# Retention followed by a leaky-ReLU MLP on one core: the front of the kernel, up to the second token group, written in another order

## The chip, the cores and the metric

The kernel runs on one core of a Trainium2 chip. The metric is device time in microseconds (us) of one execution. The profiler's trace of one execution gives the start and length of each instruction on five engines: TensorE (PE, with its weight loads shown apart as PEld), VectorE (DVE), ScalarE (ACT), GpSimd (POOL) and SyncE (SP, which here only issues DMAs). PEclk is the share of PE's full clock that was granted.

## The reference: what is computed

q, k and v are float32 tensors of 8 batches, 8 heads, 576 positions and 64 dimensions. Each head has a decay gamma. The first half is a retention layer, the second an MLP over the 4608 tokens of 512 channels:

```python
scores = scale * np.matmul(q, k.transpose(0, 1, 3, 2))
Dmat = np.where(rel >= 0, gamma[:, None, None] ** rel[None, :, :], 0.0)
ret = scores * Dmat[None, :, :, :]
return np.matmul(ret, v).astype(np.float32)
...
h = x @ w_in                      # 512 -> 2048
g = np.maximum(0.01 * h, h)
return (g @ w_out).astype(np.float32)    # 2048 -> 512
```

`rel` is the distance of two positions. x is the retention's output with the heads side by side.

## The kernel before, in words

**Units and groups.** The 4608 tokens are 36 units of 128 tokens (two chunks of 64), and 9 groups of four units (512 tokens). A batch has nine chunks, so unit 4 lies across two batches and its loads come in two halves. For a unit the kernel

- loads k, q and v with `load(u)`: three DMAs of 256 KB (pieces of 256 bytes), six of half the size for a unit across batches, into one of six sets of buffers `t32`;
- casts them to float16, q and v times decay tables (`cast_k` L165 on ACT, `cast_q` L168 and `cast_v` L172 on DVE or POOL), into `qk16` and `v16`;
- transposes k and q to `qkT`: on PE through PSUM (`transpose_pe` L193, copied out at L200 by `transposed`) for units below NPE, by a DMA on SP (`transpose_dma` L176) for later ones;
- multiplies k with q inside each chunk, and k with v for the state (`scores`, L208 and L217, 16 matmuls of 64 by 64 each, into the single PSUM tile `sc`);
- masks the scores to float16 (`masks`, L226 on DVE), adds the chunk's state to the running one (`state`, L248, L250, or L253 and L254 where the state is scaled, on DVE) and casts that to float16 (`state_cast`, L266 and L269);
- computes two output parts (`outputs`, L284 from the masked scores and L295 from the state before), 32 matmuls into different places of the single PSUM tile `ot`; `own` (L306, ACT) copies the first part to SBUF and `add` (L314, DVE) adds the second to it and writes `xT`, the MLP's input.

**The MLP of a group.** Layer 1 (L327) multiplies by `w_in` and writes g through the leaky ReLU on ACT (L341). `h_half` does two blocks of 128 hidden channels for 256 tokens, `h_block` one block for 512. Layer 2 of group 0 is `wide` (L369): 16 pieces of four 512-column matmuls, four pieces for each quarter of `w_out`. Layer 2 of the other groups is `seven` (L429), a Strassen-like scheme of seven products of 16 matmuls with 256 columns. It needs sums of weights (`mix_weights`, L394, four of them in two halves, once) and sums of g (`mix`, L413, four in two halves for each group), both on DVE. In it, `keep` (L441, L443) and `give` (L452, L454) move PSUM out, and a dictionary of hooks says what is recorded behind which product.

**What sets the order.** The order is written out by hand: each engine executes its instructions in the order in which the code records them, and a wait holds all that stands behind it on that engine. That holds for DMAs too: SP issues the unit loads, the stores and the transposes in one order, and POOL issues the weight loads (which cast to float16) between its casts. Weights come as four pieces of `w_in` (`load_w_in`, two DMAs each) and four of `w_out` (`load_w_out`). A list of earlier DMAs given as `after` makes a load wait for them. Before, the chain is: w_in 0 after unit 2 is loaded, unit 4 after w_in 2, w_out 0 after q of unit 4, unit 5 after w_out 0, w_out 2 after q of unit 5, unit 6 after w_out 2.

**The stages.** The opening (units 0 to 3), layer 1 of group 0, layer 2 of group 0 with units 4 and 5, group 1 with units 6 to 12, and then groups 2 to 8. `burst(u)` records scores of unit u and outputs of u-1, and `ahead(u)` casts and transposes a unit by DMA. `step(u)` is a burst, the load of a later unit and `ahead(u + 2)`. In groups 2 to 7 four steps lie between layer-1 blocks and products. `keep_warm` (L495) issues matmuls on zeros. They give no result.

Of the kernel before, what the change touches and what calls it, by code (L numbers as in the profile page):

```python
# [18 lines left out]
def kernel(  # L19
# [23 lines left out]
    NPE = 10  # L43
# [75 lines left out]
    def load(u, after=None):  # L119
        for x in (1, 0, 2):  # L120
# [4 lines left out]
            for j, rows in ((0, P),) if same else ((0, CH), (1, CH)):  # L125
                b, w = (c + j) // CB, (c + j) % CB
                d = nc.sync.dma_start(
# [173 lines left out]

    owns = {}
# [7 lines left out]
    def add(u):  # L310
        g, t0 = u // 4, (u % 4) * P
        if g not in xT:
            xT[g] = x_pool.tile([P, NP, TOK], F16, name="xT")
        nc.vector.tensor_tensor(  # L314
            out=xT[g][:, :, t0 : t0 + P].rearrange("q (c g) t -> q c g t", g=2),
            in0=ot_tiles[u][:, :, NP : 2 * NP].rearrange("q g (c j) t -> q c g (j t)", j=2),
            in1=owns[u].rearrange("q (c g) j t -> q c g (j t)", g=2),
            op=ADD,
        )
# [28 lines left out]
    def h_half(g, a, fb):  # L348
# [4 lines left out]
        leaky(g_tile(g)[:, 2 * fb : 2 * fb + 2, ts], hps)  # L353

# [150 lines left out]
    def prepare(u):  # L505
        cast_k(u)
        transpose_pe(u, 1)
        transposed(u, 1, nc.scalar.copy)
        cast_q(u, nc.vector)
        transpose_pe(u, 0)  # L510
        transposed(u, 0, nc.scalar.copy)
        cast_v(u, nc.gpsimd)

    def settle(u):
        state(u, 0)
        state_cast(u, nc.scalar.copy, (0,))
        masks(u)

    def settle_rest(u):
        state(u, 1)  # L520
        state_cast(u, nc.gpsimd.tensor_copy, (1,))
# [6 lines left out]
    prepare(0)  # L528
    scores(0)
    settle(0)  # L530
    w_in_loads = []
    for u in range(1, 4):
        cast_k(u)
        transpose_pe(u, 1)
        transposed(u, 1, nc.scalar.copy)
        cast_q(u, nc.vector)
        settle_rest(u - 1)
        keep_warm(2)
        transpose_pe(u, 0)
        transposed(u, 0, nc.scalar.copy)  # L540
        cast_v(u, nc.gpsimd)
        finish(u - 1)
        if u == 2:
            w_in_loads.append(load_w_in(0, (last_load[2, 2],)))
        if u == 3:
            w_in_loads.append(load_w_in(1))
        scores(u)
        settle(u)
        keep_warm(3)
    settle_rest(3)  # L550
    w_in_loads.append(load_w_in(2))
    w_in_loads.append(load_w_in(3))


    def halves(g, *items):
        for a, fb in items:
            h_half(g, a, fb)

    load(4, w_in_loads[2])
    o_loads = [load_w_out(0, (last_load[4, 0],)), load_w_out(1)]  # L560
    load(5, o_loads[0])
    o_loads += [load_w_out(2, (last_load[5, 0],)), load_w_out(3)]

    halves(0, (0, 0), (0, 1))
    finish(3)
    halves(0, (0, 2), (0, 3), (1, 0), (1, 1), (1, 2), (1, 3), (0, 4), (0, 5), (1, 4), (1, 5))
    load(6, o_loads[2])
    load(7)
    cast_k(4)
    cast_q(4, nc.vector)  # L570
    cast_v(4, nc.gpsimd)
    halves(0, (0, 6), (0, 7))
    transpose_pe(4, 1)
    transposed(4, 1, nc.scalar.copy)
    transpose_pe(4, 0)
    transposed(4, 0, nc.vector.tensor_copy)
    halves(0, (1, 6), (1, 7))
    scores(4)
    settle(4)
    settle_rest(4)  # L580
# [6 lines left out]
    load(8)  # L587
    wides((0, 1), (1, 1))
    cast_k(5)
    cast_q(5, nc.vector)  # L590
    cast_v(5, nc.gpsimd)
    wides((2, 1),)
    transpose_pe(5, 1, sc_pool)
    transposed(5, 1, nc.scalar.copy)
    transpose_pe(5, 0, sc_pool)
    transposed(5, 0, nc.vector.tensor_copy)
    wides((3, 1), (0, 2))
    scores(5)
    outputs(4)
    settle(5)  # L600
    settle_rest(5)
    own(4)
    add(4)
    wides((1, 2), (2, 2), (3, 2))
    load(9)
    finish(5)
    wides((0, 3), (1, 3), (2, 3), (3, 3))


    load(10)  # L610
    cast_k(6)
    cast_q(6, nc.vector)
    cast_v(6, nc.gpsimd)
    halves(1, (0, 0), (0, 1))
    transpose_pe(6, 1)
    transposed(6, 1, nc.scalar.copy)
    transpose_pe(6, 0)
    transposed(6, 0, nc.vector.tensor_copy)
    halves(1, (0, 2), (0, 3))
    scores(6)  # L620
    settle(6)
    settle_rest(6)
    cast_k(7)
    cast_q(7, nc.vector)
    cast_v(7, nc.gpsimd)
    load(11)
    halves(1, (0, 4))
    transpose_pe(7, 1)
    transposed(7, 1, nc.scalar.copy)
    transpose_pe(7, 0)  # L630
    transposed(7, 0, nc.vector.tensor_copy)
    halves(1, (0, 5))
    scores(7)
    outputs(6)
    settle(7)
    settle_rest(7)
    own(6)
    add(6)
    halves(1, (0, 6), (0, 7))
    finish(7)  # L640

    def pe_casts(u):
        cast_k(u)
        cast_q(u, nc.vector)
        cast_v(u, nc.gpsimd)

    def pe_transposes(u):
        transpose_pe(u, 1, sc_pool)
        transposed(u, 1, nc.scalar.copy)
        transpose_pe(u, 0, sc_pool)  # L650
        transposed(u, 0, nc.vector.tensor_copy)

    def burst(u):
# [3 lines left out]
        if u - 1 >= 8:  # L657
            outputs(u - 1)
        if u < NU:
# [3 lines left out]
            state_cast(u, nc.gpsimd.tensor_copy)  # L663
        if u - 1 >= 8:
# [3 lines left out]
    def ahead(u):  # L668

        if u < NPE or u >= NU:  # L670
            return
# [9 lines left out]
    pe_casts(8)  # L681
    pe_transposes(8)
    halves(1, (1, 0), (1, 1))
    burst(8)
    ahead(10)
    mix_weights(0, 0)
    mix_weights(0, 1)
    halves(1, (1, 4), (1, 5))
    pe_casts(9)
# [78 lines left out]
```

## Time and profile before

| | us |
|---|---|
| median of three runs (323.5 to 326.23) | 323.84 |
| the profiled execution | 323.91 |
| its span on the core | 322.1 |
| opening, to the first layer-1 matmul of group 0 | 23.4 |
| group 2 starts, in the chain of waits | 117.2 |
| one steady group | 29.1 |

The span runs from the first to the last instruction. The rest of an execution's time lies around it. In the table of windows a row is a stretch of the span: its length, then for each engine busy time with the number of instructions, then the granted clock, the mean busy share of the 16 DMA engines (which can come out over 1) and the GB/s that they wrote. In a timeline row an engine name with a q (SPq) is its queue of DMA issues, and the bracket says how long the engine had been idle and what ended that. In rows of groups the number before the comma is us in total, the one behind it the mean of one in ns, and behind the bars stands the idle time ahead of the group. In the page's part on DMA queues, q0 holds the DMAs that POOL issues, q1 those of SP; the numbers are packets, MB written and share of the 16 engines' time.

### The profile page before, as it was taken

The numbers are of one execution on the slowest core, as the hardware profiler recorded it, in microseconds if no ns is written. First come the engines' busy times: TensorE is split into PE (matmuls) and PEld (weight loads), VectorE is DVE, ScalarE is ACT, GpSimd is POOL, SyncE is SP. The second block draws the span as 40 slices with busy tenths as digits, with TensorE's granted clock in tenths as the row PEclk, the third lists the DMA queues.
The fourth block names the chain that finished last, engine by engine and source line by source line (L and its number), as shares of the span: only waits on it lengthen the run. The fifth ranks groups of instructions, "written<-read, shape, count | busy, mean of one in ns | idle before, by whom it ended". The sixth has DMA issues, their size and how long they took to land.

```text
span 322.1 us, 9343 instructions
## 1 busy us (share of the span) xinstructions
PE 283.8 (88%) x4063; PEld 192.1 (60%) x4063; DVE 171.9 (53%) x288; ACT 145.7 (45%) x255; POOL 94.7 (29%) x114
## 2 busy tenths in 40 slices
PE   2777926998757799999999999999999999999995
PEld 1345822456546664785487468647845874685474
DVE  1651002165599964783585457468636846661252
ACT  4553730136644227625732762476167237514710
POOL 1163105012257432342335333332533433000000
PEclk9997985999999999999999999999999999999999
DMA  8959698999054979769847976896597673003003
GB/s 184 220 75 174 129 207 134 222 263 243 2 132 93 190 172 242 168 137 263 184 107 166 258 166 135 163 285 156 122 263 158 147 192 123 2 4 132 0 0 132
DMA packets 149770, 49.49 MB, mean 154 GB/s; under 512 B 140640, under 2 KB 145376, under 8 KB 149728
## 3 DMA queue, kind: packets, MB, share of 16 engines
q1 hardware_dynamic: 145152, 44.58, 59.2%
q0 software_dynamic: 4288, 4.20, 8.6%
q8 instruction: 32, 0.52, 0.7%
q10 hardware_dynamic: 288, 0.11, 0.1%
q14 instruction: 10, 0.08, 0.1%
HBM read 36.81 MB, written 9.44 MB: 144 GB/s over the span
## 4 chain that ended last, share of the span: by engine, by line
PE 75%; DVE 9%; DMA 7%; ACT 3%; issue 3%; POOL 1%; SPq 1%; DVEq 0%; POOLq 0%; ACTq 0%
PE acc L327 33%; PE acc L429 28%; PE acc L369 5%; DMA t<-in_q_dram 4%; PE sc L208 2%; DMA w_in<-in_moe_w_in_dram 2%; DMA w_out<-in_moe_w_out_dram 2%; DVE w_mix L394 2%; PE sc L217 1%; PE acc L193 1%; PE ot L284 1%; PE ot L295 1%; DVE mix L413 1%; ACT qkT L200 1%; DVE s L250 1%
## 5 line engine op out<-in xcount | busy, mean ns | idle before, releaser
L327 PE MATMUL acc<-xT,w_in 128*128 128x512 f16 (+1 forms) x704 | 131.5, 344 | 2.4 <-DMA w_in<-in_moe_w_in_dram 2.4
L341 ACT ACTIVATE gt<-acc 128x512 f16<-128x512 f32 x144 | 86.1, 598 | 66.4 <-PE acc L327 64.8
L327 PEld LDWEIGHTS <-w_in 128*128 128x128 f16 x704 | 68.0, 99 | 55.9 <-issue 2.9
L429 PEld LDWEIGHTS <-gt 128*128 128x128 f16 x640 | 61.9, 98 | 13.1 <-issue 4.0
L226 DVE TENSOR_TENSOR s<-sc,cs 128x512 f16<-128x512 f32 x36 | 24.7, 686 | 46.3 <-PE sc L217 46.2
L429 PE MATMUL acc<-w_out,gt 128*128 128x256 f16 x384 | 45.9, 273 | 2.7 <-DVE v L443 1.8
L172 POOL TENSOR_TENSOR v<-t,cs 128x512 f16<-128x512 f32 x36 | 40.7, 1132 | 6.1 <-DMA t<-in_v_dram 6.1
L306 ACT COPY own<-ot 128x512 f32<-128x512 f32 x36 | 21.1, 586 | 45.9 <-PE ot L295 38.4
L266 POOL CAST st<-s 128x512 f16<-128x512 f32 x21 | 12.8, 611 | 93.7 <-DVE s L250 56.9
L429 PE MATMUL acc<-w_mix,gt 128*128 128x256 f16 x256 | 30.7, 273 | 1.0 <-DVE w_mix L394 1.0
L314 DVE TENSOR_TENSOR xT<-ot,own 128x512 f16<-128x512 f32 x36 | 24.6, 685 | 11.8 <-ACT own L306 11.7
L413 DVE TENSOR_TENSOR mix<-gt 128x1024 f16<-128x1024 f16 x16 | 15.0, 937 | 28.8 <-ACT gt L341 28.8
L429 PE MATMUL acc<-w_mix,mix 128*128 128x256 f16 x256 | 29.3, 273 | 0.0
L168 POOL TENSOR_TENSOR qk<-t,cs 128x512 f16<-128x512 f32 x26 | 28.5, 1095 | 0.0
L269 POOL CAST st<-s 128x256 f16<-128x256 f32 x15 | 6.9, 460 | 69.4 <-DVE s L254 29.0
L429 PEld LDWEIGHTS <-mix 128*128 128x128 f16 x256 | 25.1, 98 | 2.9
L165 ACT CAST qk<-t 128x512 f16<-128x512 f32 x36 | 22.3, 620 | 7.8 <-DMA t<-in_k_dram 7.8
L217 PE MATMUL sc<-v,qk 64*64 64x64 f16 x576 | 11.4, 198 | 8.9 <-POOL v L172 8.9
L250 DVE TENSOR_TENSOR s<-sc,s 128x256 f32<-128x256 f32 x40 | 16.7, 418 | 3.1 <-PE sc L217 2.6
L193 PEld LDWEIGHTS <-qk 128*128 128x128 f16 x80 | 6.0, 109 | 19.6 <-ACT qk L165 13.3
L208 PEld LDWEIGHTS <-qkT 64*64 64x64 f16 x576 | 8.4, 110 | 14.6 <-issue 12.3
L369 PE MATMUL acc<-w_out,gt 128*128 128x512 f16 x64 | 16.5, 417 | 0.0
(45 smaller groups left out, 216.8 us busy)
## 6 DMA issues: line engine op xcount, KB each, us to landing
out_dram<-osb SPq DMA_DIRECT2D x17, 512.0 KB, 3.2
t<-in_k_dram SPq DMA_DIRECT2D x32, 256.0 KB, 3.9
t<-in_q_dram SPq DMA_DIRECT2D x32, 256.0 KB, 4.3
t<-in_v_dram SPq DMA_DIRECT2D x32, 256.0 KB, 4.5
w_in<-in_moe_w_in_dram POOLq DMA_DIRECT2D x8, 256.0 KB, 5.1
w_out<-in_moe_w_out_dram POOLq DMA_DIRECT2D x4, 512.0 KB, 6.8
t<-in_k_dram SPq DMA_DIRECT2D x8, 128.0 KB, 3.3
t<-in_q_dram SPq DMA_DIRECT2D x8, 128.0 KB, 3.9
```

The source lines that it names most:

```text
L165: nc.scalar.copy(out=qk16[u][:, 1], in_=t32[u, 1])
L168: eng.tensor_tensor(out=qk16[u][:, 0], in0=t32[u, 0], in1=decay(u, 0), op=MUL)
L172: eng.tensor_tensor(out=v16[u], in0=t32[u, 2], in1=decay(u, 1), op=MUL)
L226: nc.vector.tensor_tensor(out=s16s[u], in0=sc_tiles[u][:, :, 0], in1=mask_sb.unsqueeze(1).unsqueeze(1).to_broadcast([P, 2, NP, CH]), op=MUL,)
L250: nc.vector.tensor_tensor(out=to, in0=st, in1=carry[0], op=ADD)
L306: nc.scalar.copy(out=owns[u], in_=ot_tiles[u][:, :, 0:NP].rearrange("q j c t -> q c j t"))
L314: nc.vector.tensor_tensor(out=xT[g][:, :, t0 : t0 + P].rearrange("q (c g) t -> q c g t", g=2), in0=ot_tiles[u][:, :, NP : 2 * NP].rearrang ...
L327: nc.tensor.matmul(out=hps[:, n, :], lhsT=w_in16[:, c, f * P : (f + 1) * P], rhs=xT[g][:, c, ts], start=(c == 0), stop=(c == NP - 1),)
L341: nc.scalar.activation(out=out, in_=in_, func=mybir.ActivationFunctionType.Lrelu)
L369: nc.tensor.matmul(out=ys[tb], lhsT=g_t[0][:, f, tb * P : (tb + 1) * P], rhs=w_out16[:, f, :], start=(f == 0), stop=(f == NF - 1),)
L413: nc.vector.tensor_tensor(out=z[:, fs], in0=a[:, fs], in1=b[:, fs], op=op)
L429: nc.tensor.matmul(out=r[name][:, tb, :], lhsT=lhs[:, f, tb * P : (tb + 1) * P], rhs=rhs[:, f, :], start=fresh and n == 0, stop=f == HF - ...
```

## The change

**Loads.** Units 0 to 3 stay on SP. Units 4 to 7 are issued by POOL (`load` takes an engine), in one row with the weights: w_in 3, unit 4, w_out 0 and 1, unit 5, w_out 2 and 3, units 6 and 7. The explicit order among the loads is gone but for unit 8, which waits for v of unit 6. POOL gives up the v casts of units 4 to 7, which go to DVE. w_in 0 to 2 are issued inside the opening, each behind the second state cast of its unit.

The two fences show POOL's order from the v cast of unit 3 to that of the next unit that POOL casts. `t_1`, `t_0` and `t_2` are buffers of k, q and v, the number behind them tells the tile.

Before:
```order
L172 TENSOR_TENSOR v_418<-t_2_129,cs 128x512
L143 DMA w_in_97<-in_moe_w_in_dram 64x4x512 x2
L269 CAST st_492<-s_491 128x256
L143 DMA w_in_97<-in_moe_w_in_dram 64x4x512 x4
L149 DMA w_out_98<-in_moe_w_out_dram 128x4x512 x4
L172 TENSOR_TENSOR v_700<-t_2_515,cs 128x512
```
Now:
```order
L172 TENSOR_TENSOR v_405<-t_2_129,cs 128x512
L269 CAST st_389<-s_388 128x256
L143 DMA w_in_97<-in_moe_w_in_dram 64x4x512 x2
L269 CAST st_493<-s_492 128x256 x2
L143 DMA w_in_97<-in_moe_w_in_dram 64x4x512 x2
L127 DMA t_1_504<-in_k_dram 64x8x64 x2
L127 DMA t_0_507<-in_q_dram 64x8x64 x2
L127 DMA t_2_510<-in_v_dram 64x8x64 x2
L149 DMA w_out_98<-in_moe_w_out_dram 128x4x512 x2
L127 DMA t_1_571<-in_k_dram 128x8x64
```
The cast of `v_700` (unit 4), which stood behind all four w_out loads, is no longer on POOL, and unit loads (L127) stand between the weights. Units 5 to 7 and the other w_out follow in the same way, and POOL's next cast is q of unit 8.

**Opening.** A unit's transposes are recorded ahead of the outputs of the unit before, k of the next unit is cast one step earlier, and both state casts are on POOL. The outputs of units 0 to 3 go through `outputs_acc`: both parts are accumulated in the same place of PSUM, with a drain of PE between the matmuls that read the lower and the upper 64 partitions, and one copy on ACT (`x_copy`) writes `xT`. `own` and `add` are gone for these units.

**Layer 2 of group 0 and group 1.** State casts of units 4 to 7 are both on ACT. `mix_weights` is moved up from group 1 (five halves in layer 2 of group 0, three early in group 1). Units 8 and 9 are transposed by DMA (NPE 8). In group 1 the tokens of units 6 and 7 get layer 1 by `h_unit`: four blocks of 128 channels for 128 tokens. Four steps (9 to 12) hang in `seven(1)`, behind products 0, 2, 4 and 6, where two steps (11 and 12) hung behind products 0 and 4, and a step loads unit u + 4 in place of u + 3.

ACT's order around the casts of k of units 6 (`qk_1019`, now `qk_1012`) and 7 (`qk_1121`, now `qk_1127`), before:
```order
L165 CAST qk_1019<-t_1_685 128x512
L341 ACTIVATE gt<-acc 128x2x256 x2
L200 COPY qkT<-acc 128x512
L341 ACTIVATE gt<-acc 128x2x256 x2
L269 CAST st_1112<-s_1111 128x256
L165 CAST qk_1121<-t_1_691 128x512
L341 ACTIVATE gt<-acc 128x2x256
L200 COPY qkT<-acc 128x512
```
Now:
```order
L165 CAST qk_1012<-t_1_679 128x512
L380 ACTIVATE gt<-acc 128x2x256 x2
L200 COPY qkT<-acc 128x512
L380 ACTIVATE gt<-acc 128x2x256 x3
L269 CAST st_1118<-s_1117 128x256 x2
L165 CAST qk_1127<-t_1_685 128x512
L200 COPY qkT<-acc 128x512
L380 ACTIVATE gt<-acc 128x2x256
```
Two state casts stand ahead of the cast of k of unit 7, and no layer-1 block lies between that cast and the copy of its transposes.

DVE's order at the end of `seven(1)`, from the first sum `v` (L443, now L490) to the add of unit 11 (the last L314, now L353), before:
```order
L443 TENSOR_TENSOR v<-acc,u_1804 128x512
L454 TENSOR_TENSOR osb<-acc,v 128x2x256
L226 TENSOR_TENSOR s_1910<-sc,cs 128x512
L250 TENSOR_TENSOR s_1912<-sc,s_1744 128x256
L253 TENSOR_TENSOR stmp<-sc,s_1912 128x256
L254 TENSOR_TENSOR s_1912<-stmp,cs 128x256
L314 TENSOR_TENSOR xT<-ot,own 128x4x128
L454 TENSOR_TENSOR osb<-acc,u_1804 128x2x256 x2
```
Now:
```order
L490 TENSOR_TENSOR v<-acc,u_1668 128x512
L501 TENSOR_TENSOR osb<-acc,v 128x2x256
L226 TENSOR_TENSOR s_1865<-sc,cs 128x512
L250 TENSOR_TENSOR s_1867<-sc,s_1738 128x256
L250 TENSOR_TENSOR s_1867<-sc,s_1867 128x256
L353 TENSOR_TENSOR xT<-ot,own 128x4x128
L501 TENSOR_TENSOR osb<-acc,u_1668 128x2x256 x2
L226 TENSOR_TENSOR s_1990<-sc,cs 128x512
L250 TENSOR_TENSOR s_1992<-sc,s_1867 128x256
L253 TENSOR_TENSOR stmp<-sc,s_1992 128x256
L254 TENSOR_TENSOR s_1992<-stmp,cs 128x256
L353 TENSOR_TENSOR xT<-ot,own 128x4x128
```
The last burst's masks, states and add came ahead of the last two `osb` sums and now stand behind them. The first layer-1 matmul of group 2 reads what the last row writes.

The diff, cut:

```diff
-    NPE = 10
+    NPE = 8
-    def load(u, after=None):
+    def load(u, eng=None, after=None):
...
-                d = nc.sync.dma_start(
+                d = (eng or nc.sync).dma_start(
...
+    def outputs_acc(u):
+        ot = ot_pool.tile([P, 2, 2 * NP, CH], FP, name="ot")
+        ot_tiles[u] = ot
+        to = ot[:, 0].rearrange("q (c j) t -> q c j t", j=2)
+        seen = set()
+        for r in range(2):
+            if r:
+                nc.tensor.drain()
+            for c in range(NP):
+                for o in range(2):
+                    h = c + NP * o
+                    nc.tensor.matmul(
+                        out=to[half(o), c, r, :], lhsT=v16[u][half(r), h, :],
+                        rhs=s16s[u][half(r), h % 2, h // 2, :],
+                        start=o not in seen, stop=False, skip_group_check=True,
+                    )
+                    seen.add(o)
+            for j in range(2):
+                if (2 * u + j) % CB == 0:
+                    continue
+                for c in range(r, NP, 2):
+                    for o in range(2):
+                        nc.tensor.matmul(
+                            out=to[half(o), c, j, :],
+                            lhsT=st_before(u, j)[half(r), (c + NP * o) // 2, :],
+                            rhs=qkT[u][half(r), 0, (c + NP * o) // 2, half(j)],
+                            start=False, stop=True, skip_group_check=True,
+                        )
+    def x_copy(u):
+        nc.scalar.copy(
+            out=x_of(u), in_=ot_tiles[u][:, 0].rearrange("q (c j) t -> q c (j t)", j=2)
+        )
...
+    def h_unit(u, fb):
+        g, t0 = u // 4, (u % 4) * P
+        ts = slice(t0, t0 + P)
+        hps = acc_pool.tile([P, 4, P], FP, name="acc")
+        for n in range(4):
+            h_mm(hps, n, g, 4 * fb + n, ts)
+        leaky(g_tile(g)[:, 4 * fb : 4 * fb + 4, ts], hps)
...
+    for u in range(3):
+        n = u + 1
+        state(u, 0)
+        state_cast(u, pool_copy, (0,))
+        transpose_pe(n, 1)
+        transposed(n, 1, act_copy)
+        keep_warm(1)
+        cast_q(n, nc.vector)
+        masks(u)
+        state(u, 1)
+        cast_v(n, nc.gpsimd)
+        state_cast(u, pool_copy, (1,))
+        load_w_in(u)
+        transpose_pe(n, 0)
+        transposed(n, 0, act_copy)
+        keep_warm(2)
+        outputs_acc(u)
+        x_copy(u)
+        if n < 3:
+            cast_k(n + 1)
+        keep_warm(1)
+        scores(n)
+        if u:
+            keep_warm(2)
...
+    load_w_in(3)
+    load(4, nc.gpsimd)
+    load_w_out(0)
+    load_w_out(1)
...
+    halves(1, (0, 3), (0, 4))
+    scores(6)
+    settle(6)
+    pe_casts(7)
+    turn(7, 1)
+    halves(1, (0, 5))
+    turn(7, 0)
+    ahead(8)
+    load(10)
...
-    seven(1, {0: [lambda: step(11)], 1: [rest_of_weights], 4: [lambda: step(12)]})
+    seven(
+        1,
+        {
+            0: [lambda: step(9)],
+            2: [lambda: step(10)],
+            4: [lambda: step(11)],
+            6: [lambda: step(12)],
+        },
+    )
```

`turn(u, x)` is the two PE transposes calls of before in one function, `settle(u)` records both chunks' states, state casts (ACT) and the masks, `pe_casts(u)` the three casts.

244 lines of the change are left out of this document (95 added, 149 removed).

## The prediction

> **What bounds the kernel now.** I read the page first, for where TensorE (PE) is not busy, then a table of stages, then who waits inside the bad stages, then the DMA.
>
> ```profile
> span 322.1 us, 9343 instructions
> ...
> PE   2777926998757799999999999999999999999995
> ...
> PEclk9997985999999999999999999999999999999999
> ...
> q1 hardware_dynamic: 145152, 44.58, 59.2%
> q0 software_dynamic: 4288, 4.20, 8.6%
> ```
>
> The span is 322.1 us. The 40 slices are about 8 us each: from slice 16 on PE is full, and the holes and the low clocks lie in the first fifteen, up to about 117 us. The table of windows puts numbers on the stages: the opening, layer 1 of group 0, the hole, layer 2 of group 0, all of group 1, then one steady group.
>
> ```profile
> core 0: us, PE busy (x) PEld busy (x) DVE busy (x) ACT busy (x) POOL busy (x), PEclk, DMA share, GB/s
> 0.00:23.38 23.38, 13.21 (x271) 7.73 (x271) 9.79 (x22) 11.29 (x21) 8.03 (x15) 1.00 0.77 163
> 23.38:42.60 19.22, 17.03 (x184) 14.18 (x185) 3.07 (x6) 10.89 (x20) 4.31 (x7) 0.91 0.90 149
> 42.60:51.90 9.30, 0.36 (x16) 0.30 (x16) 0.00 (x0) 0.99 (x2) 2.55 (x3) 0.67 0.92 163
> 51.90:70.03 18.13, 17.46 (x175) 7.94 (x168) 6.42 (x12) 2.58 (x5) 3.10 (x4) 0.89 1.08 223
> 70.03:117.19 47.16, 35.29 (x691) 29.09 (x690) 38.46 (x60) 21.01 (x38) 18.82 (x19) 1.00 0.66 145
> 117.19:146.30 29.11, 29.07 (x433) 19.36 (x432) 17.05 (x30) 14.95 (x26) 11.20 (x14) 1.00 0.80 184
> ```
>
> A steady group costs 29.11 us with PE busy for 29.07 of it, so group 2 onward is bound by PE, and the change leaves that alone. Group 1 takes 47.16 us, with PE idle for 11.9. Between 42.60 and 51.90 PE does 0.36 us of work. The timeline tells why:
>
> ```profile
> 44.08 0.58 SPq L127 DMA_DIRECT2D t<-in_q_dram  x1
> 48.93 1.48 POOL L149 DMA_DIRECT2D w_out<-in_moe_w_out_dram  x2 [9.49 <-DMA t<-in_q_dram]
> 50.42 1.06 POOL L172 TENSOR_TENSOR v<-t,cs 128x512 f16<-128x512 f32 x1
> 51.54 0.43 PE L217 MATMUL sc<-v,qk 64*64 64x64 f16 x16 [8.95 <-POOL v L172]
> 51.90 8.23 PE L369 MATMUL acc<-w_out,gt 128*128 128x512 f16 x28
> ```
>
> PE waits 8.95 us for POOL's cast of v of unit 4. POOL is held in front of it by w_out loads that wait for a load of unit 5. PE then runs cold (clock 0.67 and 0.89 in these two stages). So the end is set by PE, and what can be won is PE's waits before 117.
>
> **The change part by part.** I rebuild the front by hand, with durations from these rows (the chain of waits, then groups by form, then DMA by window).
>
> ```profile
> 66.85 3.56 PE acc L369 x16
> 70.41 1.75 PE acc L327 x16
> 72.15 0.45 PE acc L193 x8
> 107.89 4.19 DVE w_mix L394 x4
> 113.53 3.65 PE acc L429 x32
> 117.19 4.32 PE acc L327 x20
> ```
> ```profile
> L172 POOL TENSOR_TENSOR v<-t,cs 128x512 f16<-128x512 f32 x36 | 40.7, 1132 | 6.1 <-DMA t<-in_v_dram 6.1
> L226 DVE TENSOR_TENSOR s<-sc,cs 128x512 f16<-128x512 f32 x36 | 24.7, 686 | 46.3 <-PE sc L217 46.2
> L314 DVE TENSOR_TENSOR xT<-ot,own 128x512 f16<-128x512 f32 x36 | 24.6, 685 | 11.8 <-ACT own L306 11.7
> L165 ACT CAST qk<-t 128x512 f16<-128x512 f32 x36 | 22.3, 620 | 7.8 <-DMA t<-in_k_dram 7.8
> L306 ACT COPY own<-ot 128x512 f32<-128x512 f32 x36 | 21.1, 586 | 45.9 <-PE ot L295 38.4 <-DVE osb L454 5.4
> L250 DVE TENSOR_TENSOR s<-sc,s 128x256 f32<-128x256 f32 x40 | 16.7, 418 | 3.1 <-PE sc L217 2.6
> L143 POOL DMA_DIRECT2D w_in<-in_moe_w_in_dram x8 | 5.1, 650 | 0.0
> L149 POOL DMA_DIRECT2D w_out<-in_moe_w_out_dram x4 | 3.0, 755 | 19.9 <-DMA t<-in_q_dram 19.9
> L269 ACT CAST st<-s 128x256 f16<-128x256 f32 x7 | 2.8, 404 | 8.7 <-DVE s L250 6.7 <-DVE s L248 1.2 <-DVE s L254 0.8
> ```
> ```profile
> 2.00:14.00 12.00, 6.02 (x117) 3.73 (x117) 3.78 (x8) 5.69 (x11) 2.44 (x3) 1.00 1.05 239
> 26.00:32.00 6.00, 4.16 (x24) 3.10 (x25) 0.69 (x1) 1.62 (x3) 1.53 (x3) 0.73 1.14 174
> 62.00:70.00 8.00, 8.00 (x129) 3.80 (x127) 4.35 (x8) 1.99 (x4) 1.40 (x2) 1.00 1.12 253
> ```
>
> *DMA.* A unit is 0.786 MB in float32: 3.3 us at 239 GB/s, 3.1 at 253. Half a million weights land as 0.524 MB of float16: 3.0 us at 174 GB/s, for each of the eight weight pieces. With all of it in order and no gaps: units 0 to 3 from 2.0 take 13.2 us, to 15.2. The new order issues w_in 0 and 1 at about 11 and 16 (each behind POOL's state cast of its unit), beside the loads of units 2 and 3. By the shares and counts above a packet of the hardware queue costs 21 ns (59.2% of 322.1 us on 16 engines over 145152 packets) and one of the software queue, so far weights alone, 103. No row shows the two queues loaded together, so unit 3 lands between 15.2 (weights last) and 21.2 (both pieces first); I take 21.2, the end that hurts. The third piece stands behind POOL's v cast of unit 3, so it starts at 22. From there, back to back: w_in 2 and 3 to 25 and 28, unit 4 to 31.1, w_out 0 and 1 to 34.1 and 37.1, unit 5 to 40.3, w_out 2 and 3 to 43.3 and 46.3, unit 6 to 49.4, unit 7 to 52.5.
>
> The Trainium skill (DMA: Bandwidth & Descriptors, Queues, rings and completion order) says that each DMA engine goes round the queues that have work, packet by packet. By that rule packets of 103 ns alternate with packets of 21, the weights get five sixths of the time while both have work, and the sum stays at its 21.2 end; were the queues served by bytes, unit 3 would land some 1.5 us earlier and the sum would be 302.5. No trace of the kernel before shows which.
>
> *Opening.* It drops an own copy (586 ns on ACT) and the add (685 on DVE) for one copy on ACT, moves the state casts to POOL and adds a PE drain per unit (nothing like it in the trace: 0 to 0.2 us, one 64-column matmul, hidden by the wait for unit 3). With arrivals as above the end is v of unit 3 at 21.2, POOL's cast 1.1, the second half of its scores 0.3: 22.6, against 23.38 before.
>
> *Layer 1, group 0.* 16 halves of 8 matmuls at 1.75/16 us: 14.0. Outputs of unit 3 0.75, eight transposes 0.45, scores of unit 4 0.35, joints 0.4: 38.5. All w_in is there by 28, and PE, not idling, needs no cold start.
>
> *The hole* is gone: v of unit 4 is cast on DVE (an op like the 686 ns one), with unit 4 there at 31.1 and DVE idle. Late next could be w_out 0, needed at 38.5 and there at 34.1. Further on: w_out 1 needed at 42.4 (37.1), unit 5 at 44 (40.3), w_out 2 at 47 (43.3), w_out 3 at 50.5 (46.3), unit 6 at 54 (49.4), unit 7 at 61.5 (52.5). The least slack is 3.5 us.
>
> *Layer 2, group 0.* 16 pieces of four 512-column matmuls (3.56/16 each): 14.2; outputs of 4 and 5, transposes of 5, scores of 5: 1.5; joints 0.5: ends at 54.7, against 70.03.
>
> *Group 1.* Eight halves 7.0. Sixteen transposes 0.9. Scores and outputs of 6 and 7 and scores of 8: 1.75 (0.7 for each set of scores and outputs: a steady group, 29.11 less 64 times 4.32/20 less 112 times 3.65/32, leaves 0.63 for each of its four). The 128 matmuls with 128 columns in place of 64 with 256: 7.2 at 0.45/8 each, as much as before. Seven products of 16 matmuls at 3.65/32 are 12.8, with four bursts 2.8 inside. Sum 32.4. Waits, as the new orders of ACT and DVE have them: transposes of 7 stand directly behind the scores of 6, and their k cast stands on ACT behind two state casts and on DVE three w_mix halves and the states: 3.3. Unit 6's add before its first layer-1 block 0.4. DVE's masks behind the mixes, and one transpose DMA, 1.8. At the end the outputs of unit 11 come behind the last product, so own, give, masks, scaled state and add (0.59+0.69+0.69+1.3+0.69, partly together) stand between them and group 2: 2.9. Not placed 1.5, for small waits of the kind that leave PE idle for 11.9 us in this stage now. Sum 9.9, so group 2 starts at 97.0. The 4.19 us of w_mix on the old chain are moved into layer 2, where DVE has room (6.42 busy of 18.13).
>
> *Sum.* Group 2 started at 117.19 less the 0.2 by which its first row is merged late, 117.0. Gain 20.0; span 302.1; the profiled run was 323.91 for a span of 322.1, so 303.9, say **304.0** us. The profiled run lies 0.07 us from the median of 323.84.
>
> **The rivals.**
>
> (a) *The four bursts inside group 1 wait for their transposes.* They come every 3.7 us against 7.3 in a steady group, each needs POOL's two casts (1.1 each), and its DMA transpose stands on SP's queue behind a unit's load of 3.1 us. If bursts 10, 11 and 12 each wait for one such load: 9.3 us, 313.3. For it: the DMA share here would be near full. Against: loads are issued a unit earlier than before.
>
> (b) *Generating 1024 descriptors in software is slow.* A w_in piece has 256 and takes POOL 650 ns; in proportion a load takes 2.6 us, a unit 7.8 in place of 3.1, and unit 7 lands at 71.3, 9.8 behind its need: 313.8. Against: w_out has 512 and takes 755, and POOL's cast at 50.42 began right after two of them and took its usual 1.06. The Trainium skill (DMA: Bandwidth & Descriptors, Anatomy of one DMA) also holds that many descriptors can be emitted before their cost shows; by that (b) falls away.
>
> (c) *The other side: the software queue pays by packet, not by byte.* A unit is 192 packets per engine. At 103 ns, the software queue's packet so far, it takes 19.8 us, units 4 to 7 are 67 us late in sum, unit 7 lands at 119 and is needed at 61.5: about 362, slower. It decides at 54 ns a packet, 10.4 us a unit, where the gain of 20 and the slack of 9 are gone. Against: those 103 ns are for packets that read 2 KB, four to eight times as much; the hardware queue moves 256 bytes in 21.
>
> (d) *The work is only moved.* The hole was also time in which DMA was 0.92 busy: if order, not amount, was all that changed, the wait for v becomes one for w_out or unit 6, and group 1 gives the rest back, as (a) and (b) together would: 323. Against: the DMA share was 0.24 from 16 to 20 and 0.38 from 22 to 24, which the earlier issue fills.
>
> ```profile
> 16.00:20.00 4.00, 2.95 (x72) 1.67 (x70) 1.97 (x4) 2.22 (x5) 2.70 (x4) 1.00 0.24 31
> 22.00:24.00 2.00, 1.76 (x40) 0.98 (x26) 1.74 (x4) 0.64 (x2) 1.27 (x3) 1.00 0.38 52
> ```
>
> **How the numbers follow.** Forecast 0.57, (a) 0.15, (b) 0.11, (c) 0.09, (d) 0.04, other losses 0.04 that leave it slower or equal in halves. The forecast's own range is 298 to 309: 1.5 down if unit 3 lands early, 3 to 4 down if the unplaced waits and half of group 1's do not come; 5 up for as much again of waits. The range that holds 8 in 10 takes in (a) and (b): 297 to 314.5. About 1% (3.2 us) is what a measurement can tell from no change: faster by more than that is the forecast, (a) and (b), with a part of the rest, 0.85; within it 0.05; slower 0.10.
>
> **What would show it.** Right: no wait of PE for POOL's v near scores of unit 4; PE's clock at 1.00 from about 22 us; layer 2 starting near 38.5; group 1 near 55; group 2 near 97; steady groups still 29.1. (a) would show as PE's L208 waiting for the transpose DMA; (b) as long POOL rows on the load's line; (c) as a DMA share near 1 with GB/s far under 200 between 28 and 60; unit 3's landing as the wait of POOL's third v cast. It is wrong if units 4 to 7 land later than needed, or if group 1 keeps its 47 us.

## The result, and the profile after

| | before | after |
|---|---|---|
| median, us | 324.56 (323.5 to 326.23, 4 runs) | 311.41 (309.61 to 312.65, 4 runs) |
| ratio to before | | 0.9586, 95% interval 0.9517 to 0.9654 |
| the profiled execution, us | 323.91 | 312.65 |
| its span | 322.1 | 310.9 |
| scores of unit 4 (end of layer 1 of group 0) | 42.3 | 38.25 (forecast 38.5) |
| group 1 starts | 70.0 | 54.98 (forecast 54.7) |
| group 2 starts | 117.2 | 102.84 (forecast 97.0) |

The change saves 13 us where 20 were forecast. 311.41 lies inside the range of 297 to 314.5 that takes in rivals (a) and (b), but outside the forecast's own range of 298 to 309. In the profile the first 55 us came out as worked out, and the whole gain lies there: group 1 starts 15.0 us earlier. Group 1 was to become 4.9 us shorter and became 0.7 longer (47.86 us for 47.16), and group 2 takes 2.8 us more than a steady group.

The page of the kernel after: PE and granted clock in 40 slices, and the DMA queues.

```profile
PE   1989999759966799999999999999999999999994
...
PEclk9999999969999599999999999999999999999999
...
q1 hardware_dynamic: 134736, 41.95, 57.8%
q0 software_dynamic: 5296, 7.34, 12.2%
```

The hole of before (slices 5 and 6, counted from 0) is filled. Two dips are left, in slices 7 and 8 and in 11 to 13, and the last slice of each has a low clock (0.6 and 0.5). By stage (length; busy time of PE, PEld, DVE, ACT, POOL; clock; DMA share; GB/s):

```profile
0.00:22.80 22.80, 14.51 (x265) 8.07 (x266) 8.39 (x19) 10.10 (x17) 10.06 (x19) 1.00 0.94 190
22.80:38.70 15.90, 15.81 (x202) 13.74 (x201) 3.23 (x7) 10.76 (x19) 13.46 (x20) 1.00 1.05 170
38.70:54.98 16.28, 15.89 (x169) 7.50 (x170) 10.03 (x18) 4.26 (x9) 4.42 (x5) 1.00 1.01 249
54.98:102.84 47.86, 35.74 (x737) 30.52 (x736) 32.67 (x54) 20.51 (x38) 16.59 (x17) 0.91 0.81 177
102.84:134.70 31.86, 31.83 (x433) 20.05 (x433) 16.39 (x28) 14.94 (x26) 11.66 (x15) 0.92 0.85 193
```

Layer 1 and layer 2 of group 0 now follow each other with PE idle for 0.5 us in 32. Group 1 takes 47.86 us against the 42.3 forecast: PE is idle for 12.1 (forecast 9.9) and busy for 35.74 (forecast 32.4). Group 2 takes 31.86 where a steady group takes 29.1. PE's timeline gives the waits of group 1, and the first row of group 2:

```profile
65.38 0.61 PE L193 MATMUL acc<-ident,qk 128*128 128x128 f16 x4 [5.06 <-ACT qk L165]
65.78 1.91 PE L366 MATMUL acc<-xT,w_in 128*128 128x256 f16 x8
...
88.25 0.32 PE L208 MATMUL sc<-qkT 64*64 64x64 f16 x16 [1.95 <-DVE s L250]
94.28 0.32 PE L208 MATMUL sc<-qkT 64*64 64x64 f16 x16 [1.48 <-DMA qkT<-qk]
99.74 0.32 PE L208 MATMUL sc<-qkT 64*64 64x64 f16 x16 [1.15 <-DMA qkT<-qk]
102.84 7.08 PE L366 MATMUL acc<-xT,w_in 128*128 128x512 f16 x20 [2.39 <-DVE xT L353]
```

These five waits are 12.0 of the 12.1 us. The first 20 matmuls of group 2 take 7.08 us; where PE comes to them at full clock, in a run below, the same row has 4.48. Windows from 64 us on, late in the first of these waits, and one behind the last show why:

```profile
64.00:66.00 2.00, 0.62 (x6) 0.56 (x7) 1.57 (x4) 0.92 (x2) 0.00 (x0) 0.50 0.01 4
66.00:68.00 2.00, 2.00 (x13) 1.56 (x12) 0.00 (x0) 0.85 (x2) 0.00 (x0) 0.50 0.03 8
68.00:70.00 2.00, 2.00 (x28) 1.22 (x29) 0.42 (x1) 0.97 (x3) 0.00 (x0) 0.50 0.00 0
70.00:72.00 2.00, 2.00 (x75) 1.57 (x64) 0.70 (x2) 1.52 (x3) 0.00 (x0) 0.85 0.65 148
...
104.00:106.00 2.00, 2.00 (x6) 0.73 (x5) 0.00 (x0) 0.60 (x1) 0.93 (x1) 0.50 1.09 367
```

The clock is at half for six to seven us at each, from within the wait on. At half clock half of PE's busy time is lost: 0.3, 1.0 and 1.0 us in the three windows from 64, 0.3 more from 70 to 72, so 2.6 there, and group 2's 31.86 us are 2.8 more than a steady group's 29.1. **The cold clock costs 5.4 us, and no term of the sum stood for it.**

### The profile page after: what moved, and what is told of

The parts are those of the page before. It is cut to its first block, busy times and chain, and to the rows that moved or that the text cites. A ratio compares the mean times of both kernels' runs of the same rounds, so it can differ in the third digit from the quotient of the medians.

```text
span 310.9 us, 9426 instructions
## 1 busy us (share of the span) xinstructions
PE 285.1 (92%) x4104; PEld 193.5 (62%) x4104; DVE 167.8 (54%) x284; ACT 144.5 (46%) x253; POOL 102.8 (33%) x127
## 4 chain that ended last, share of the span: by engine, by line
PE 74%; DMA 12%; DVE 7%; SPq 3%; POOL 1%; issue 1%; ACT 0%; DVEq 0%; ACTq 0%
PE acc L366 37%; PE acc L476 28%; DMA w_out<-in_moe_w_out_dram 4%; SPq L127 3%; DMA t<-in_v_dram 3%; DMA qkT<-qk 3%; PE acc L416 2%; PE sc L208 2%; DMA w_in<-in_moe_w_in_dram 2%; PE ot L284 1%; PE sc L217 1%; DVE w_mix L441 1%; PE ot L295 1%; DVE mix L460 1%; DVE s L226 1%
## 5 line engine op out<-in xcount | busy, mean ns | idle before, releaser
L366 PE MATMUL acc<-xT,w_in 128*128 128x512 f16 (+2 forms) x768 | 134.7, 333 | 2.4 <-DVE xT L353 2.4
L366 PEld LDWEIGHTS <-w_in 128*128 128x128 f16 x768 | 70.0, 100 | 56.8 <-issue 5.9
L348 ACT COPY own<-ot 128x512 f32<-128x512 f32 x32 | 18.7, 585 | 52.2 <-PE ot L295 45.2
L172 POOL TENSOR_TENSOR v<-t,cs 128x512 f16<-128x512 f32 x32 | 35.2, 1099 | 9.5 <-DMA t<-in_v_dram 9.5
L168 POOL TENSOR_TENSOR qk<-t,cs 128x512 f16<-128x512 f32 x28 | 30.1, 1076 | 9.7 <-DMA t<-in_q_dram 9.7
L353 DVE TENSOR_TENSOR xT<-ot,own 128x512 f16<-128x512 f32 x32 | 21.9, 683 | 8.4 <-ACT own L348 8.4
L165 ACT CAST qk<-t 128x512 f16<-128x512 f32 x36 | 22.4, 621 | 0.4 <-DMA t<-in_k_dram 0.4
L193 PE MATMUL acc<-ident,qk 128*128 128x128 f16 x56 | 7.2, 270 | 12.2 <-ACT qk L165 9.2
L208 PE MATMUL sc<-qkT 64*64 64x64 f16 x576 | 11.7, 200 | 5.3 <-DMA qkT<-qk 2.6
L501 DVE TENSOR_TENSOR osb<-acc,u 128x512 f32<-128x512 f32 (+1 forms) x17 | 11.1, 656 | 8.6 <-PE acc L476 8.6
```

What stands on the lines that cost most here:

```text
L165: nc.scalar.copy(out=qk16[u][:, 1], in_=t32[u, 1])
L168: eng.tensor_tensor(out=qk16[u][:, 0], in0=t32[u, 0], in1=decay(u, 0), op=MUL)
L172: eng.tensor_tensor(out=v16[u], in0=t32[u, 2], in1=decay(u, 1), op=MUL)
L208: nc.tensor.matmul(out=a[half(j), g, 0, p, :], lhsT=qkT[u][half(g), 1, p, half(j)], rhs=qkT[u][half(g), 0, p, half(j)], start=True, stop=T ...
L348: nc.scalar.copy(out=owns[u], in_=ot_tiles[u][:, :, 0:NP].rearrange("q j c t -> q c j t"))
L353: nc.vector.tensor_tensor(out=x_of(u).rearrange("q (c g) t -> q c g t", g=2), in0=ot_tiles[u][:, :, NP : 2 * NP].rearrange("q g (c j) t -> ...
```

## The experiments

Each run's ratio is to runs of the kernel before on the same chip.

**Is the hole, on its own, worth its 9 us?** The kernel before with one cast moved:

```diff
-    cast_v(4, nc.gpsimd)
+    cast_v(4, nc.vector)
```

> The kernel before, with one edit: the v cast of unit 4 is on DVE and no longer behind POOL's w_out loads. Theory (the hole at 42.6 was an order of POOL, and is most of the gain): layer 2 of group 0 starts when w_out 0 is there, at 43.7 in place of 51.9, w_out 2 then holds PE for some us, and PE does not go cold: 8 to 9 us less, 315.5 to 316.5. Rival (the hole was DMA time, the wait only changes its name): at most 3 us less, 321 or more. If the theory holds, the rest of the change is worth 4 to 5 us of the 13.

Measured 320.39 us, ratio 0.9882 (0.9834 to 0.9929). Its chain of waits (start, length, what):

```profile
38.02 5.83 DMA w_out<-in_moe_w_out_dram
...
44.30 5.12 DMA t<-in_q_dram
...
49.95 5.76 DMA w_out<-in_moe_w_out_dram
```

The wait of 8.95 us for v is gone, and waits for w_out, 4.9 us in sum, take more than half of its place: each load waits for the one before it. The hole alone is worth 3.3 us (323.66 us on the same chip for the kernel before), nearer the rival. Rival (d) of the prediction is what happens when only the cast is moved.

**Is it the single GpSimd queue?** The kernel after with units 4 to 7 on SP again, in the same order, kept by waits:

```diff
-    load(4, nc.gpsimd)
-    load_w_out(0)
+    load(4, after=w_in_loads[2])
+    w0 = load_w_out(0, (last_load[4, 1],))
...
-    load(5, nc.gpsimd)
-    load_w_out(2)
+    load(5, after=w0)
+    w2 = load_w_out(2, (last_load[5, 1],))
...
-    load(6, nc.gpsimd)
-    load(7, nc.gpsimd)
+    load(6, after=w2)
+    load(7)
```

> The changed kernel with units 4 to 7 issued by SP in the same order, each load or weight behind an earlier one by a wait (unit 4 behind w_in 2, w_out 0 behind k of unit 4, unit 5 behind w_out 0, w_out 2 behind k of unit 5, unit 6 behind w_out 2). Theory (the order counts, and the slack of 3 us and more covers a slower queue): 311 to 312.5. Rival (the one queue is what wins, since it is never empty and moves small pieces faster): layer 2 of group 0 waits for w_out 2 or 3, 313.5 or more.

Measured 316.65 us, ratio 0.9753 (0.9706 to 0.9799): some 5 us of the gain are gone, as the rival had it. Its chain again has one transfer waiting for another, and layer 2 waits for w_out (PE's timeline, below it):

```profile
34.08 5.95 DMA w_out<-in_moe_w_out_dram
...
40.05 4.68 DMA t<-in_k_dram
...
45.26 5.77 DMA w_out<-in_moe_w_out_dram
```
```profile
51.07 1.89 PE L416 MATMUL acc<-w_out,gt 128*128 128x512 f16 x8 [2.65 <-DMA w_out<-in_moe_w_out_dram]
```

In the kernel after that wait is 0.39 us, at 47.11. From 24 to 56 us the DMA moves less here at the same share of busy time (this run, then the kernel after):

```profile
24.00:56.00 32.00, 29.26 (x328) 19.97 (x330) 9.69 (x19) 13.93 (x25) 4.90 (x8) 0.98 1.00 173
```
```profile
24.00:56.00 32.00, 31.52 (x368) 21.09 (x367) 13.00 (x24) 14.84 (x27) 16.72 (x22) 1.00 1.05 217
```

So the one queue keeps the order without a wait between transfers. Group 2 starts 4.8 us later here than in the profile of the kernel after: 2.2 of that come in layer 2 of group 0 with the wait for w_out, 0.8 in group 1, and 1.8 before the scores of unit 4, where profiles of one and the same code differ by more (see the part on why the prediction was right or wrong). This run changes the queue and the waits together, so it doesn't tell how much is due to each.

**What does each queue do by itself?** A kernel of loads alone, which computes nothing and writes zeros: three units on SP, then three on GpSimd, then two on SP beside two w_in pieces on GpSimd.

> A measurement that computes nothing (it writes zeros): three units loaded by SP alone, then three by GpSimd alone, then two units on SP beside two pieces of w_in on GpSimd. Theory (GpSimd's queue moves the 256-byte pieces in larger packets and so faster): about 3.2 us a unit from SP (240 to 255 GB/s), at most 2.6 from GpSimd (over 300 GB/s), in about a twelfth of the packets. Rival (both queues move them alike, and the 320 GB/s seen with the changed kernel come from the mix with weights): 3.1 to 3.3 us in both. In the third stage, if the engines take turns by packet the weights land well ahead of the units (within 7 to 8 us of the start, the units at about 12); by bytes all end together.

On SP the three units have landed at 13.9 us, at a steady 218 GB/s; on GpSimd the steady rate is 217. So the rival holds that both queues move the pieces alike, at some 3.6 us a unit (0.786 MB at 218 GB/s); larger packets are not faster. A load's issue takes POOL 0.91 us. Third stage (DVE reads one column of each load as it lands):

```profile
28.18 2.50 POOL L143 DMA_DIRECT2D w_in<-in_moe_w_in_dram  x4 [5.96 <-DMA t<-in_v_dram]
...
36.15 0.15 DVE L555 COPY sink<-t 128x1 f32<-128x1 f32 x1 [4.97 <-DMA t<-in_q_dram]
...
40.88 0.15 DVE L555 COPY sink<-t 128x1 f32<-128x1 f32 x1 [4.58 <-DMA t<-in_v_dram]
41.88 0.15 DVE L555 COPY sink<-t 128x1 f32<-128x1 f32 x1 [0.85 <-DMA t<-in_k_dram]
```

While the weights are in flight one tensor of a unit takes 5 us; alone it takes 1.2, and afterwards 1.0. So beside weights the SP queue moves at about a quarter of its pace. The weights land 6.5 to 10.3 us after their issue, unit 7 some 13 us after the stage's start and unit 8 some 16: the order that was forecast for turns by packet, each later than forecast. That speaks for the end that the prediction took (unit 3 last, behind two weight pieces), and it is what the one queue avoids for units 4 to 7. The Trainium skill (DMA: Bandwidth & Descriptors, Queues, rings and completion order) has each DMA engine go round its queues packet by packet; the quarter agrees with it in kind, though the prediction had worked out a sixth from it.

**Is the PSUM sum worth anything?** The kernel after with outputs, own and add for units 0 to 3:

```diff
-        outputs_acc(u)
-        x_copy(u)
+        finish(u)
...
-    outputs_acc(3)
-    x_copy(3)
+    finish(3)
```

> The changed kernel with outputs of units 0 to 3 as before (two parts of PSUM, own on ACT, add on DVE) in place of the sum in PSUM; all else stays. Theory (the opening is bound by the landing of unit 3, POOL's v cast of it starts at 20.95): 311 to 312, no change. Rival (the sum in PSUM shortens the chain of every unit): own and add return to the chain three times, 313.5 or more.

Measured 311.39 us, ratio 0.9601 (0.9541 to 0.9661): no difference, as the theory had it. The sum in PSUM brings nothing that these runs can tell. That the landing of unit 3 alone ends the opening is not shown: in two runs below (zeros in the gaps, and unit 7's casts moved ahead) POOL's v cast of unit 3 starts at 19.6, 1.3 us earlier than in the kernel after, and layer 1 still starts at 23.0 and 22.6.

**The clock.** The kernel after with matmuls on zeros in the first and in the last gap of group 1:

```diff
     pe_casts(7)
+    keep_warm(22)
...
-            6: [lambda: step(12)],
+            6: [lambda: step(12), lambda: keep_warm(10)],
```

> The changed kernel with matmuls on zeros in the two long waits of PE: 22 ahead of the transposes of unit 7, 10 behind the last product of group 1. No wait is taken away. Theory (after each of the two waits PE runs at half clock, which costs 2.2 us in the halves behind the first and 2.8 us in group 2's first layer-1 blocks): 306 to 307.5, and the first 20 matmuls of group 2 take 4.3 us in place of 7.1. Rival (the clock's loss is absorbed by later waits, or the matmuls are slow for another reason): 310.5 or more.

Measured 308.4 us, ratio 0.9515 (0.9469 to 0.9561). The halves behind the transposes of 7, and the first row of group 2:

```profile
65.11 1.04 PE L366 MATMUL acc<-xT,w_in 128*128 128x256 f16 x8
...
85.45 0.32 PE L208 MATMUL sc<-qkT 64*64 64x64 f16 x16 [1.95 <-DVE s L250]
86.53 3.26 PE L476 MATMUL acc<-w_mix,mix 128*128 128x256 f16 x16
...
101.27 4.48 PE L366 MATMUL acc<-xT,w_in 128*128 128x512 f16 x20
```

The eight matmuls take 1.04 us in place of 1.91, the 20 take 4.48 in place of 7.08: a wait's second price, paid after it, is real. Of 5.4 us about 3 come back, less than the theory's 4 to 5. Part is lost again to waits, and a product behind the untouched wait for DVE runs cold (3.26 us). In the kernel after the same product behind the same wait of 1.95 us ran at full clock:

```profile
89.14 1.92 PE L476 MATMUL acc<-w_mix,mix 128*128 128x256 f16 x16
```

Seven profiles have this wait, at 1.94 or 1.95 us. Behind it the clock stayed at 1.00 in four (the kernel after, and the runs with units 4 to 7 on SP, without the PSUM sum and with unit 7's casts ahead) and went to 0.50 in three (this run, and those with POOL's casts held and with step 12 behind product 5). So the length of a wait alone does not tell whether the clock falls.

**The wait for the transposes of unit 7.** First, POOL's casts of units 8 and 9 are held until DVE's w_mix halves are done. In the kernel after, and then in this run, DVE's three halves:

```profile
58.59 0.94 DVE L441 TENSOR_TENSOR w_mix<-w_out,w_mix 128x1024 f16<-128x1024 f16 x1
59.44 1.53 DVE L441 TENSOR_TENSOR w_mix<-w_out 128x1024 f16<-128x1024 f16 x1
60.89 1.57 DVE L441 TENSOR_TENSOR w_mix<-w_out,w_mix 128x1024 f16<-128x1024 f16 x1
```
```profile
60.88 0.68 DVE L441 TENSOR_TENSOR w_mix<-w_out,w_mix 128x1024 f16<-128x1024 f16 x1
61.48 0.68 DVE L441 TENSOR_TENSOR w_mix<-w_out 128x1024 f16<-128x1024 f16 x1
62.09 0.68 DVE L441 TENSOR_TENSOR w_mix<-w_out,w_mix 128x1024 f16<-128x1024 f16 x1
```

```diff
-        cast_q(u, nc.gpsimd)
+        c = cast_q(u, nc.gpsimd)
+        if u == 8:
+            behind(c, last_mix)
...
-        mix_weights(n, 1)
+        last_mix = mix_weights(n, 1)
```

> The changed kernel with POOL's casts of units 8 and 9 held until the last of the three w_mix halves is done. Theory (these halves, 0.94, 1.53 and 1.57 us, are slowed by the casts that run on POOL at the time): 0.7 us each, PE's wait at the transposes of 7 falls from 5.06 to about 3.1: 309 to 310. Rival (the halves are slow by themselves): no change in them.

Measured 311.58 us, ratio 0.9577 (0.9518 to 0.9635): the time did not move. The cause of the slow halves is shown all the same: with POOL still, they take 0.68 us, and the wait at the transposes is 3.64 instead of 5.06, after which the halves of layer 1 run warm:

```profile
66.27 0.40 PE L193 MATMUL acc<-ident,qk 128*128 128x128 f16 x4 [3.64 <-ACT qk L165]
66.50 1.04 PE L366 MATMUL acc<-xT,w_in 128*128 128x256 f16 x8
```

The sharing moved on, though: POOL's held casts now ran beside DVE's v cast of unit 7, which took 1.52 us in place of 0.68. Group 1 is 3.1 us shorter in this profile (57.27 to 102.03). But the scores of unit 4 came at 41.16, 2.9 us later than in the kernel after: layer 1 started 1.7 us later, and its first 16 matmuls, with the clock at 0.50 from 24 to 26 us, took 3.07 us in place of 1.91. That hides the gain in this profile. Whether the timed runs lost it in the same way, no trace shows.

Second, the casts of unit 7 are moved ahead of two halves of layer 1, and the w_mix halves behind the masks of 6:

```diff
-    for n in range(1, 4):
-        mix_weights(n, 1)
+    pe_casts(7)
     halves(1, (0, 3), (0, 4))
     scores(6)
     settle(6)
-    pe_casts(7)
+    for n in range(1, 4):
+        mix_weights(n, 1)
```

> The changed kernel with the three casts of unit 7 moved ahead of the scores of unit 6, and the three w_mix halves behind the states of unit 6. Theory (the k cast of 7 was late only because of what stood ahead of it on ACT and DVE): PE's wait of 5.06 us at the transposes of 7 falls under 0.5 and the half clock behind it goes: 6 to 7 us less, 304.5 to 306. Rival (given back inside the seven products, where DVE is full): 309 or more, with longer waits of the bursts.

Measured 306.98 us, ratio 0.9487 (0.9443 to 0.953). The wait of 5.06 is gone, with the cold clock behind it, and group 2 starts 5.3 us earlier; the time is 1 us above the theory's range. The other four waits remain, next to small new ones ahead of them (the longest 1.04 us, for the add of unit 6):

```profile
82.54 0.32 PE L208 MATMUL sc<-qkT 64*64 64x64 f16 x16 [1.95 <-DVE s L250]
89.06 0.32 PE L208 MATMUL sc<-qkT 64*64 64x64 f16 x16 [1.97 <-DMA qkT<-qk]
94.47 0.32 PE L208 MATMUL sc<-qkT 64*64 64x64 f16 x16 [1.10 <-DMA qkT<-qk]
97.58 6.16 PE L366 MATMUL acc<-xT,w_in 128*128 128x512 f16 x20 [2.39 <-DVE xT L353]
```

**The end of group 1.** The kernel after with the step of unit 12 behind product 5:

```diff
-            6: [lambda: step(12)],
+            5: [lambda: step(12)],
```

> The changed kernel with step 12 behind product 5 in place of 6. Theory (the burst of 12 is held by its DMA transpose, which lands at 99.7, not by its place): PE now waits some 3 us for that transpose behind product 5, and group 2 starts at most 0.5 us earlier: 310.5 to 311.5. Rival (the wait of 2.39 for the add of unit 11 and the half clock behind it come from the place alone, as the prediction had it): 306 to 307.

Measured 309.82 us, ratio 0.9539 (0.9501 to 0.9576). The wait for the add goes and one for the transpose DMA of unit 12 comes (3.07 us at 98.82); group 2 starts at 102.46, 0.4 us earlier, but warm: its first 20 matmuls take 4.48 us. Group 2 wins the clock, not the wait; the product behind the new wait runs cold in its place (2.81 us). The time lies between the two forecasts, and 1.6 us below the kernel after is within what these intervals leave open.

**Together.** The order of the second run on unit 7, unit 12's step behind product 5, and the casts and transposes of units 11 to 14 asked for one unit earlier; then the same with six matmuls on zeros behind the last product:

```diff
+    ahead(11)
...
-            0: [lambda: step(9)],
-            2: [lambda: step(10)],
-            4: [lambda: step(11)],
-            6: [lambda: step(12)],
+            0: [lambda: step(9, 3)],
+            2: [lambda: step(10, 3)],
+            4: [lambda: step(11, 3)],
+            5: [lambda: step(12, 0)],
```

> The order in which the transposes of unit 7 find their cast done (the wait of 5.06 us gone, as in the run that moved the cast of unit 7 ahead), with the casts and DMA transposes of units 11 to 14 asked for one unit earlier and the twelfth unit's step one product earlier. If the waits left in group 1 are for transposes that are asked for late, the waits of 1.97 and 1.10 us before the scores of units 10 and 11 go, the one of unit 12 (3.07 us when its step stood behind product 5 with the old request) goes too, group 2 starts at 94 to 95.5 us and its first 20 matmuls take 4.3 to 4.8 us instead of 6.16: 302 to 304 us in all. If the engines that feed them are full there (VectorE with sums, masks and states, GpSimd with casts), the waits change their name to masks and states, group 2 starts at 97 us or later and the time is 306 us or more.

> The same with six matmuls of nothing behind the last product of group 1, in the wait for unit 12's add. If the TensorE clock at the start of group 2 still costs something there, the first 20 matmuls of group 2 come down to 4.3 to 4.5 us and the time is 0.5 to 1.5 us below the one without them; if the clock is at full speed there already (because the wait is under 2.5 us), it is within 0.3 us or later by the length of the six, 0.3 to 0.7 us.

Measured 304.7 us, ratio 0.9411 (0.9365 to 0.9458), and 306.36 us, ratio 0.9441 (0.9397 to 0.9485). The first beats the kernels before and after; it lies between its two forecasts, and its interval overlaps that of the order with unit 7's casts ahead (0.9443 to 0.953), so that what the rest adds is not certain. The six matmuls add nothing that these runs can tell: the first 20 of group 2 take 4.48 us in both. In the second's profile group 2 starts at 95.91. PE's longest waits in its group 1 (us in total, times, longest):

```profile
PE sc L208 <- DVE s L250: 3.0, 1, 3.0
PE acc L366 <- DVE xT L353: 1.0, 1, 1.0
```

No wait for a transpose DMA is left, as expected. What grew is the wait for DVE, 1.95 to 3.0: POOL's four casts of 10 and 11 now all run beside DVE's sums of g, and four of these take twice their time, where two did in the kernel after.

```profile
75.21 1.52 DVE L460 TENSOR_TENSOR gt<-gt 128x1024 f16<-128x1024 f16 x1
76.66 1.53 DVE L460 TENSOR_TENSOR mix<-gt 128x1024 f16<-128x1024 f16 x1
78.22 1.42 DVE L460 TENSOR_TENSOR mix<-mix,gt 128x1024 f16<-128x1024 f16 x1
79.56 1.53 DVE L460 TENSOR_TENSOR gt<-gt 128x1024 f16<-128x1024 f16 x1
```

**The same casts, earlier.** POOL's casts of 10 and 11 ahead of the burst of unit 8:

```diff
+    ahead(10)
+    load(12)
     h_unit(7, 0)
     h_unit(7, 2)
+    ahead(11)
     burst(8, False)
-    ahead(10)
-    load(12)
-    ahead(11)
```

> The same order with POOL's casts of units 10 and 11 recorded ahead of the burst of unit 8, and so ahead of POOL's cast of unit 8's state, behind which POOL stood idle for 11.9 us while VectorE had nothing to share with it; until now these four casts (1.5 us each) ran beside VectorE's eight sums of g, of which four took 1.42 to 1.53 us in place of 0.7. If that sharing is what makes PE wait 3.0 us for the masks and states of unit 9 before the scores of unit 10, the sums take 0.7 to 0.8 us each, that wait shrinks to under 0.7 us, group 2 starts 2.3 to 3 us earlier than in the run before it and the time is 301 to 302.5 us. If VectorE is late there by its own count of work, or the casts of 10 and 11 now wait for their loads and hold the state cast of unit 8, the wait stays at 2.5 us or moves to the scores of 9, and the time is 304 us or more.

Measured 305.38 us, ratio 0.9436 (0.9384 to 0.9487): no gain. POOL's timeline:

```profile
77.36 1.34 POOL L168 TENSOR_TENSOR qk<-t,cs 128x512 f16<-128x512 f32 x1 [3.69 <-DMA t<-in_q_dram]
```

The cast of unit 11 waits for its load, the state cast of unit 8 stands behind it, and PE waits for that:

```profile
81.00 0.26 PE L295 MATMUL ot<-qkT,st 64*64 64x64 f16 x8 [3.90 <-POOL st L269]
```

This is the rival: the state cast of unit 8 is held, as it said. The wait for DVE is gone and the first four sums take 0.7 us, but the later ones still meet the late cast of unit 11. In this order the loads of group 1 seem to be the next limit; asking for them earlier wasn't tried.

## Why the prediction was right or wrong

**Opening: right in this profile.** POOL's third v cast began at 20.95, waiting for unit 3 (forecast 21.2), and the second half of its scores ended at 22.4 (22.6).

**Layer 1, the hole, layer 2: right.** Scores of 4 at 38.25, group 1 at 54.98 against 54.7. One arrival was late, w_out 2 at 47.07 for 43.3; its slack took all but 0.39 us.

That these times agree to 0.3 us is in part luck. Eight profiles here share the code up to the scores of unit 4, and these come between 38.06 and 42.19. In the latest (the first run of the part called Together) the first 16 matmuls of layer 1 took 3.51 us in place of 1.91, though the row of the granted clock reads 1.00 there; so 1.00 in the opening does not prove a warm PE.

**Group 1: not shortened.** It was to take 42.3 us, and it took 47.86. The prediction had named this as a sign that it is wrong ("if group 1 keeps its 47 us"). So the 4.9 us forecast here did not come, and 0.7 went, with 2.8 more at the start of group 2.

**Group 1's waits: the kinds right, the sizes 2.1 us short.** Transposes of 7: 3.3 forecast, without its parts being told, and 5.06 measured; DVE's halves took up to 1.57 us there beside POOL's casts, and with the casts held the wait was 3.64. Masks and one transpose DMA 1.8 and not placed 1.5: measured 1.95, 1.48 and 1.15. The 1.5 had no wait of its own behind it, so that part of it was needed is chance. The add at the end: 2.9 forecast, 2.39 measured. Unit 6's add: 0.4 forecast, none.

The Trainium skill (SBUF — State Buffer, SBUF: two separate sides) says that a DVE operation with two SBUF inputs and a GpSimd operation that reads SBUF hold one pair of ports by turns. The 0.68 and 1.53 us of the same operation agree.

**The clock: the step that failed.** The prediction said that PE, not idling, needs no cold start in layer 1, and that the clock would be 1.00 from about 22 us on. It then put waits of up to 3.3 us into group 1, 9.9 in sum, and priced each at its own length alone. The rows of before stood in its own tables, 0.67 in the hole and 0.89 in the stage behind it. Measured: 2.6 us behind the first wait, 2.8 at the start of group 2. The Trainium skill (TensorE: Matmul & The Clock Gate, What's actually happening) has the clock fall to half after an idle window of some 3.4 us, whose start is free-running. Here it fell in a wait of 5.06, and not in one of 3.64. It fell also at group 2 after gaps of 1.15 and 2.39 us with 0.7 us of matmuls between, and in three of seven profiles at a wait of 1.95 us. So in these runs waits shorter than 3.4 us dropped the clock, and the same wait did so in one profile and not in another; where a window began, no trace shows.

**The sum.** The profiled run is 8.65 us over the forecast: 0.3 at the start of group 1; in group 1 idle time 2.2 and busy time 3.3 more, of which 2.6 are the clock and 0.7 stay unexplained; 2.8 in group 2.

**Rivals.** (a) came in part: PE waited for transposes before units 11 and 12, 1.48 and 1.15 us and not 3.1 each. (b) fell: a load's issue took 0.9 us. (c) fell: 217 GB/s alone. Its premise was wrong by a factor of twelve: the queue's packets rose by 1008 for 3.14 MB more, 3.1 KB or twelve pieces each, where it had one packet for each piece. (d) did not happen for the whole change, but did for one of its parts. The prices of (a) and (b), 313.3 and 313.8, are nearer to the measured time than the forecast's 304, but neither is what happened. The prediction's "half a million weights" are 262144; the 0.524 MB that it counts with are right.

## What to carry to other kernels

Price a wait of TensorE of some 2 us or more twice: by its length, and by the cold matmuls that may follow it, up to 3 us here. Waits of about 2 us had this second price in some profiles only, the one of 3.64 us had none. Filling the waits with matmuls on zeros won back some 3 us here, and reordering so that the longest went away won some 4. When a stall is removed alone, the next transfer in a chain of waits can take its place (3.3 us won of 9); with the order kept by one queue and no waits, the gain came. Compare stages, and not only the start of a late one, since up to the scores of unit 4 the same code took up to 4 us more in one profile than in another. Where work is moved to a free stretch of VectorE, look at what GpSimd does in the same stretch.

## What had not been expected of the hardware

One queue of plain 256-byte pieces ran at 217 GB/s from GpSimd and at 218 from SP. GpSimd's packets held twelve pieces each. Beside weights that are cast on the way, SP's loads fell to about a quarter of their pace. The same operation on VectorE took 0.68 us alone and 1.53 beside GpSimd's casts. The same wait of 1.95 us left TensorE's clock at 1.00 in four profiles and brought it to 0.50 in three others.
